# Value products placed after half a chunk more, both heads' probabilities in one tile, and a planner that repeats itself by latest times

## The chip, the cores and the metric

One Trainium2 core (of a chip with eight) runs the whole program. The metric is the device time of one execution in microseconds (us); lower is better.

## The reference

Sliding-window attention with a few global keys feeds a two-layer network with ELU between the layers; everything is 32-bit on input and output (the weights arrive as 64-bit numbers).

```python
scores = q @ k.T / sqrt(64) - slope[h] * dist        # B=4, H=8, S=768, D=64
keep   = (key < 8) | (0 <= query - key < 96)
a      = softmax(where(keep, scores, -1e9))
x      = concat_heads(a @ v)                          # 3072 x 512
h      = x @ w_in                                     # 512 -> 2048
g      = where(h > 0, h, exp(min(h, 0)) - 1)
out    = g @ w_out                                    # 2048 -> 512
```

## The kernel before, in words

**Tiling.** The 3072 tokens are twelve groups of 256, counted 0 to 11. A group has four head pairs for attention. The inner width 2048 is sixteen chunks of 128. Groups 0 to 2 run the network chunk by chunk while the weights are being converted (`moe`, L679), and groups 0 to 3 run attention in plain fp32 (`pair32`, L619). From group 3 on the network goes through `moe7` (L752): eight double chunks, each with an "up" (24 products of 128x256, L747, an accumulator of one PSUM bank) and a "down" (21 products, L808, seven block products in place of eight, each in three passes). `w_in` is streamed again from DRAM for each group, four loads of 512 KB in a period, through SP's queue into a ring of four slots.

**Split numbers.** Operands are split in a high part (rounded to fp32r) and a low part (the rest), so that two passes follow every tile: a copy (L282 when on ACT, L284 elsewhere) and a subtraction (`minus`, L290). All of them show the lines of these helpers, so the tile name tells them apart.

**The steady stretch.** While groups 3 to 10 run the network, attention of groups 4 to 11 is done beside it, one pair in a period of two double chunks (`pair`, L427). For pair k the steps are:
- load of q, v (`rqv`, L459) and keys (`rk`, L460), one buffer each;
- split of q (`qs`: ACT L482, DVE L484), of the keys (`ks`) and of v (`vd`: GpSimd L284 and L290). `vd` has two slots, so `vd` of pair k+2 waits for the value products of pair k; and as it is the last reader of `rqv`, the next load of `rqv` waits for it;
- a "visit" (L567), one unit on TensorE: the transposes of pair k-1 (L525, into the banks `t` and `th`) and the scores of pair k (L505, into the banks s0 and s1);
- softmax: mask and row maximum on DVE (L594, it frees the banks s0 and s1), exp on ACT (L596), the sum's reciprocal on DVE (L609, L610), scaling on DVE (L582);
- after the transposes: `pt`, high part on ACT (L282) and low part on DVE (L290), for each of two banks and two heads: four passes each;
- value products (L554), eight in a pair; their result goes through `x` (ACT L282, DVE L561) into `xh`.

The banks s0 and s1 hold in turn the accumulator of the even up, of the odd up and the two score tiles, so an up waits for the softmax of the visit ahead of it and a visit for the ELU passes (ACT L675, L676, DVE L677) of the ups.

**Order.** A planner, `Plan.order` (L106), lists every unit for every engine at build time, from costs written beside the units (`act`, `dve`, `pool`, L215 to L231) and a model of load times (`BW`, `LAT`, L62). An engine takes what can start now, the earliest `due` first. Where a unit has several engines (`alts`), the one that ends it first is taken. A flag `port` keeps certain DVE passes and all GpSimd passes from overlapping in the plan. Units with a `seq` run on TensorE exactly in the order of that number. On the chip each engine runs its list strictly in order, waiting where an input is late. In the steady stretch the numbers are offsets in a period of 13200 (constants at L914): up of the even chunk 0, values 2890, up of the odd chunk 3840, down of the previous odd chunk 6730, visit 9250, down of the even chunk 10650.

**End of a group.** When the last down of a group is done, `fin` (L824 to L830) gathers its four accumulators; the next group's first down writes the same banks.

The change touches `Op`, `Plan.add`, two new methods of `Plan`, `pair`, `inverse`, `norm`, `moe7`, `build`, the constants and `run`.

Of the kernel before, what the change touches and what calls it, by code (L numbers as in the profile page):

```python
# [53 lines left out]
class Op:  # L54
    __slots__ = ("room", "alts", "emit", "reads", "writes", "due", "n", "deps", "outs", "ready", "eng", "start", "end", "allocs", "uses", "bytes", "slack", "floor", "seq")


class Plan:
# [16 lines left out]
    def add(self, alts, emit, reads=(), writes=(), due=0.0, after=(), nbytes=0, slack=0.0, floor=0.0, seq=None):  # L75
# [11 lines left out]
        op.deps = len(deps)  # L87
# [16 lines left out]
    BY_DUE = ("S",)  # L104

# [113 lines left out]
def act(n, psum=False, extra=0.0):  # L219
    return (("ACT", (55 if psum else 97) + 0.834 * n + extra, False),)  # L220
# [14 lines left out]
class Kernel:  # L235
# [191 lines left out]
    def pair(self, b, gi, hp, xh, xl, due, ahead, step, X):  # L427
# [54 lines left out]
        p.add(act(W), lambda e: nc.scalar.activation(qs.t[:, HI], q32(), AF.Copy, scale=sc), [rqv], [qs], ahead - 4000)  # L482
# [8 lines left out]
        p.add(pool(nv, False), lambda e: self.copy(e, vv()[:, :, 0::3, :], v32()[:, v0:]), [rqv], [vd], due - 8000, self.parted)  # L491
        p.add(pool(nv), lambda e: self.minus(e, vv()[:, :, 1:3, :], v32()[:, v0:], vv()[:, :, 0::3, :]),
# [20 lines left out]
        self.inverse(st, ahead + 4500 + 3 * step)  # L513
# [13 lines left out]
        def rest():  # L527
            pts = [self.sb("pt", "pt", [P, 2 * NT, 2, P], F32R) for _ in range(2)]
            d = due - 2000
            for x, tp in enumerate(tps):  # L530
                r = slice(64 * x, 64 * x + 64)
                for j, pt in enumerate(pts):
                    if t0:
                        cut = [(slice(0, HK), slice(0, 4))]
                    else:
                        cut = [(slice(0, kr), slice(2 * i + a0, 2 * i + 2)) for i, (_, _, _, a0, kr, _) in enumerate(tiles)]
                    for rows, c in cut:
                        n = (c.stop - c.start) * 64
                        src = lambda j=j, tp=tp, rows=rows, c=c: tp.t[rows, 4 * j + c.start:4 * j + c.stop]
                        hi = lambda pt=pt, rows=rows, c=c, r=r: pt.t[rows, c, HI, r]  # L540
                        lo = lambda pt=pt, rows=rows, c=c, r=r: pt.t[rows, c, LO, r]
                        p.add(act(n, True), lambda e, src=src, hi=hi: self.copy(e, hi(), src()), [tp], [pt], d + 2 * x + j)
                        p.add(dve(n), lambda e, src=src, hi=hi, lo=lo: self.minus(e, lo(), src(), hi()), [tp, pt], [pt], d + 500 + 2 * x + j)
            self.after = []
# [3 lines left out]
            for j, pt in enumerate(pts):  # L548
                pv = self.bank("pv", "pv", [P, NT, 2, P])

                def values(e, j=j, pt=pt, pv=pv):
                    for i, (_, _, _, a0, kr, _) in enumerate(tiles):
                        for a in range(a0, 2):
                            nc.tensor.matmul(pv.t[:, i].rearrange("p s w -> p (s w)"), vd.t[:kr, 2 * i + a, j].rearrange("p s d -> p (s d)"),  # L554
                                             pt.t[:kr, 2 * i + a].rearrange("p s w -> p (s w)"), start=a == a0, stop=a == 1)

                self.after.append(p.add((("PE", 119.0 * sum(2 - x[3] for x in tiles), False),), values, [vd, pt], [pv], due + j, slack=0.0 if X.get("seven") else self.BEHIND, seq=due + j if X.get("seven") else None))
                r, o = head[j], head[1 - j]
                p.add((("ACT", 385.0, False),), lambda e, pv=pv, r=r, o=o: self.copy(e, xt(r), pv.t[o, :, 0]), [pv], [x], due + 500 + j)
                for y in range(2):  # L560
                    p.add(dve(W), lambda e, pv=pv, r=r, y=y: nc.vector.tensor_tensor(xt(r), pv.t[r, :, y], xt(r), ALU.add), [pv, x], [x], due + 600 + 2 * y + j)  # L561
            p.add(act(W), lambda e: self.copy(e, xh.t[:, HI, hp], x.t), [x], [xh], due + 700)
            p.add(pool(W), lambda e: self.minus(e, xh.t[:, LO, hp], x.t, xh.t[:, HI, hp]), [x, xh], [xl], due + 800)
# [41 lines left out]
    def inverse(self, st, due):  # L605
        nc = self.nc
# [5 lines left out]
        self.plan.add((("DVE", 290.0, False),), inverse, [st], [st], due)  # L612

    def norm(self, pr, lo, st, i, due, both):
        n = WN - lo
        self.plan.add((act(n, extra=90) + pool(n, False) if both else ()) + (("DVE", 130 + 0.53 * n, True),), lambda e: self.scaled(
            e, pr.t[:, lo:], pr.t[:, lo:], st.t[:, 2, i:i + 1]), [pr, st], [pr], due)

    def pair32(self, b, hp, t0, q32, k32, v32, rqv, rk, pv, due, step, X):  # L619
# [20 lines left out]
        self.inverse(st, d - 3500)  # L640
# [111 lines left out]
    def moe7(self, rows, xh, xl, up_at, down_at):  # L752
# [8 lines left out]
        def up(c, d):  # L761
            h = self.bank("S", "h", [P, 2, W], self.LAST_H if final and c >= N7 - 2 else None)
            for j in range(2):
# [6 lines left out]
                self.three(h, lambda j=j: h.t[:, j], w1, xh, xl, d + 10 * j, True)  # L770
            z = self.sb("z", "z", [P, 8, P], slots=["xh2"] if rows == self.GS * W and c == 1 else None)
            e = d + 2800
# [4 lines left out]
            any_ = lambda n: dve(n, port=True)  # L777
            tt = lambda e, out, x, y, op: self.on(e).tensor_tensor(out, x, y, op)  # L778
# [5 lines left out]
            ends = dve(3 * P, port=True) if final and c >= N7 - 2 else ()  # L784
            p.add(pool(3 * P) + ends, lambda e: self.minus(e, gg.t[:, LO, :3], z.t[:, 1:4], gg.t[:, HI, :3]), [z, gg], [low[0]], e)
# [32 lines left out]
        e = down_at[-1] - 4000  # L818
        fin = self.sb("fin", "fin", [P, 8, half], slots=["xh2"])
        lower = p.tile(None, "lower", None)  # L820
# [3 lines left out]
        p.add(act(DM, True), lambda _: nc.scalar.copy(f(5, 2), acc[0].t.rearrange("p i w -> p (i w)")), [acc[0]], [fin], e)  # L824
        p.add(dve(DM), lambda _: v(fin.t[:, 0:2], acc[1].t, twice(6), ALU.add), [acc[1], fin], [fin], e + 1)
        p.add(dve(DM), lambda _: v(fin.t[:, 2:4], acc[2].t, twice(0), ALU.add), [acc[2], fin], [fin], e + 2)
        p.add(dve(half), lambda _: v(f(4), acc[2].t[:, 0], f(3), ALU.add), [acc[2], fin], [lower], e + 3)
        p.add(dve(half), lambda _: v(f(3), f(3), f(5), ALU.subtract), [fin], [lower], e + 4)
        p.add(act(half, True), lambda _: nc.scalar.copy(f(7), acc[3].t[:, 0]), [acc[3]], [fin], e + 2)  # L829
        p.add(dve(half), lambda _: v(f(2), f(7), f(2), ALU.add), [fin], [fin], e + 5)  # L830
        end = down_at[-1] + 3000
        self.store(rows + P, [fin], lambda: f(1, 2), end)
        self.store(rows, [fin, lower], lambda: f(3, 2), end, final)

    def build(self):
# [52 lines left out]
        for (n, f0, f1), d in zip(segs, dues):  # L888
            def moe(n=n, f0=f0, f1=f1, d=d):
                b, gi = groups[n]  # L890
                rows = b * self.S + gi * W
                if n >= self.GS:
                    period = lambda c: d[0] + c // 2 * self.PERIOD
                    if n == len(groups) - 1:
# [5 lines left out]
                              [period(c) + (self.PERIOD + self.DOWN if c % 2 else self.VISIT + 1400.0) for c in range(self.NF7)])  # L900
# [7 lines left out]
        for _, f in sorted(todo, key=lambda x: x[0]):  # L908
# [5 lines left out]
    PERIOD, SECOND, DOWN, VISIT, AFTER = 13200.0, 3840.0, 6730.0, 9250.0, 20040.0  # L914
# [7 lines left out]
    ATT = {0: (0.0, 20000.0), 1: (20000.0, 36000.0), 2: (36000.0, 56000.0)}  # L922
# [5 lines left out]
             "pr": ["pr0", "pr1", "pr2", "pr3"], "st": [f"st{i}" for i in range(6)], "pt": ["pt0", "pt1"],  # L928
# [278 lines left out]
```

## Time and profile before

| | |
|---|---|
| three runs, median (lowest to highest) | 708.02 us (704.05 to 709.47) |
| the profiled execution, own time | 704.28 us |
| its span, first to last instruction | 702.5 us |
| TensorE busy, share of the span | 664.3 us, 95% |
| VectorE (DVE) | 588.1 us, 84% |
| ScalarE (ACT) | 483.4 us, 69% |
| GpSimd (POOL) | 293.3 us, 42% |
| bytes moved by DMA | 137.75 MB, 196 GB/s |

The rows below come from this execution. "x8" behind a row is a count; in a timeline neighbours of one kind are merged into one row. A bracket such as [1.42 <-DVE pt L290] is the idle time of the engine just before the instruction and what ended it. PEld is TensorE's weight load, SPq the queue of SyncE that issues loads and stores. PEclk is the granted TensorE clock as a share of full speed.

### The profile page before, as it was taken

The page shows a single profiled execution, that of the slowest core. Times are in us where ns is not written, and L with a number is a line of the kernel's source. Part 1 is how long each engine was busy: PE and PEld are TensorE (multiplying, and loading weights), DVE is VectorE, ACT ScalarE, POOL GpSimd, SP SyncE. Part 2 cuts the span into 40 slices and gives each one's busy share as a digit, 9 for nine tenths or more (in the row PEclk, how much of TensorE's full clock was granted, in tenths as well). Part 3 has the DMA queues.
Part 4 walks back from the last instruction along what each step waited for, and adds up shares of the span by engine and source line. Part 5 has one row for each costly group of instructions (what it writes and reads, how often), then busy time and mean ns, then how long its engine had stood idle before and what let it go on. Part 6 is the DMA issues. An engine that isn't in the chain of part 4 may idle for free.

```text
span 702.5 us, 16143 instructions
## 1 busy us (share of the span) xinstructions
PE 664.3 (95%) x5710; PEld 616.6 (88%) x5710; DVE 588.1 (84%) x1699; ACT 483.4 (69%) x1324; POOL 293.3 (42%) x307
## 2 busy tenths in 40 slices
PE   8999999999999998999999999999999899999995
PEld 6778888888789988999899889989998899989995
DVE  8999999999999879878778798787978887976644
ACT  7998887757686766567667576766767667765442
POOL 3152000203335544554455545444554455445440
PEclk9999999999999999999999999999999999999998
DMA  7838949311187564665656656755764766555651
GB/s 259 297 101 308 377 177 385 139 41 42 50 254 235 182 184 162 223 222 191 203 176 197 223 160 223 242 175 195 241 208 155 225 195 222 187 168 193 221 171 35
DMA packets 47627, 137.75 MB, mean 196 GB/s; under 512 B 5170, under 2 KB 14130, under 8 KB 47538
## 3 DMA queue, kind: packets, MB, share of 16 engines
q1 hardware_dynamic: 47248, 136.24, 57.6%
q8 instruction: 47, 0.77, 0.4%
q10 hardware_dynamic: 290, 0.39, 0.2%
q14 instruction: 42, 0.34, 0.1%
HBM read 119.84 MB, written 16.78 MB: 194 GB/s over the span
## 4 chain that ended last, share of the span: by engine, by line
PE 48%; DVE 20%; DMA 15%; ACT 12%; issue 3%; POOL 1%; SPq 1%; ACTq 0%; DVEq 0%; POOLq 0%
PE h L747 22%; DMA rqv<-in_qkv_dram 14%; PE a L808 12%; ACT pr L596 5%; PE o L705 4%; PE pv L554 4%; DVE pt L290 3%; DVE st L609 2%; ACT pt L282 2%; DVE pr L594 2%; DVE z L778 1%; PE s L505 1%; DVE g L409 1%; DVE gl L290 1%; DVE g L387 1%
## 5 line engine op out<-in xcount | busy, mean ns | idle before, releaser
L290 POOL TENSOR_TENSOR gg<-z,gg 128x384 fp32r<-128x384 f32 (+1 forms) x140 | 166.7, 1201 | 147.1 <-ACT gg L282 145.0
L747 PE MATMUL h<-xh,w0s 128*128 128x256 f32 x1728 | 218.4, 283 | 0.2
L747 PEld LDWEIGHTS h<-xh,w0s 128*128 128x128 f32 x1728 | 211.6, 192 | 0.8 <-DVE nmax L594 0.8
L808 PE MATMUL a<-w,gg 128*128 128x256 f32 x864 | 140.2, 277 | 0.1
L282 ACT CAST gg<-z 128x384 fp32r<-128x384 f32 (+1 forms) x144 | 81.2, 565 | 56.1 <-DVE z L677 32.5
L808 PEld LDWEIGHTS a<-w,gg 128*128 128x128 f32 x864 | 118.8, 188 | 0.4 <-ACT fin L829 0.3
L778 DVE TENSOR_TENSOR z<-z 128x128 f32<-128x128 f32 (+1 forms) x216 | 98.3, 456 | 3.0
L596 ACT ACTIVATE pr<-pr,nmax 128x232 f32<-128x232 f32 (+1 forms) x192 | 90.4, 472 | 14.8 <-DVE nmax L594 14.8
L747 PEld LDWEIGHTS h<-xh,w 128*128 128x128 f32 x576 | 82.2, 189 | 9.7 <-issue 1.7
L747 PE MATMUL h<-xh,w 128*128 128x256 f32 x576 | 89.0, 285 | 0.2
L594 DVE CUSTOM_DVE_ANT_0 pr<-s,tab 128x232 f32<-128x232 f32 (+1 forms) x192 | 64.6, 374 | 28.8 <-PE s L505 28.7
L677 DVE SCALAR_TENSOR_TENSOR z<-z,h 128x512 f32<-128x512 f32 x72 | 49.3, 685 | 34.1 <-ACT z L676 15.6
L675 ACT ACTIVATE z<-h 128x512 f32<-128x512 f32 x72 | 43.0, 598 | 49.6 <-PE h L747 47.4
L808 PE MATMUL a<-ta,gg 128*128 128x256 f32 x432 | 71.5, 277 | 0.0
L554 PE MATMUL pv<-pt,vd 116*128 116x256 f32 (+1 forms) x240 | 40.8, 297 | 23.1 <-DVE pt L290 22.3
L705 PE MATMUL o<-w,gh 128*128 128x512 f32 x192 | 59.4, 401 | 1.3 <-DVE ob L732 0.5
L561 DVE TENSOR_TENSOR x<-pv,x 64x256 f32<-64x256 f32 x128 | 53.8, 421 | 7.9 <-ACT x L282 4.8
L808 PEld LDWEIGHTS a<-ta,gg 128*128 128x128 f32 x432 | 59.3, 188 | 0.2 <-ACT gg L282 0.2
L554 PEld LDWEIGHTS pv<-pt,vd 116*128 116x128 f32 (+1 forms) x240 | 32.4, 190 | 29.7 <-issue 14.5
L808 PE MATMUL a<-tb,gg 128*128 128x256 f32 x216 | 50.0, 292 | 0.0
L582 DVE TENSOR_SCALAR pr<-pr,st 128x232 f32<-128x232 f32 (+1 forms) x143 | 47.3, 388 | 0.2
L584 POOL TENSOR_SCALAR pr<-pr,st 128x232 f32<-128x232 f32 (+1 forms) x31 | 17.2, 566 | 71.2 <-PE o L705 25.9
(131 smaller groups left out, 1169.3 us busy)
## 6 DMA issues: line engine op xcount, KB each, us to landing
w0s<-kept SPq DMA_DIRECT2D x144, 512.0 KB, 4.5
rqv<-in_qkv_dram SPq DMA_DIRECT2D x45, 384.0 KB, 4.7
rk<-in_qkv_dram SPq DMA_DIRECT2D x45, 184.0 KB, 3.2
bits<-in_w_in_dram SPq DMA_DIRECT2D x16, 512.0 KB, 6.5
bits<-in_w_out_dram SPq DMA_DIRECT2D x16, 512.0 KB, 9.1
kept<-w SPq DMA_DIRECT2D x16, 512.0 KB, 5.3
out_dram<-fin SPq DMA_DIRECT2D x17, 256.0 KB, 2.4
kept<-w SPq DMA_DIRECT2D x8, 256.0 KB, 5.2
```

The lines of the kernel that those rows point to most:

```text
L282: self.nc.scalar.copy(out, x)
L290: self.on(e).tensor_tensor(out, x, y, ALU.subtract)
L554: nc.tensor.matmul(pv.t[:, i].rearrange("p s w -> p (s w)"), vd.t[:kr, 2 * i + a, j].rearrange("p s d -> p (s d)"), pt.t[:kr, 2 * i + a].r ...
L561: p.add(dve(W), lambda e, pv=pv, r=r, y=y: nc.vector.tensor_tensor(xt(r), pv.t[r, :, y], xt(r), ALU.add), [pv, x], [x], due + 600 + 2 * y + j)
L582: self.nc.vector.tensor_scalar(out, x, sc, None, ALU.mult)
L594: p.add((("DVE", 158 + 1.042 * n, False),), lambda e: nc.vector.tensor_tensor_reduce(pr.t[:, lo:], st_()[:, lo:], tab, -(2.0 ** -(h + 1)), ...
L596: p.add(act(n, extra=200), lambda e: nc.scalar.activation(pr.t[:, lo:], pr.t[:, lo:], AF.Exp, bias=nm, scale=-1.0, accum_out=st.t[:, 0, i: ...
L677: p.add(dve(n), lambda e: nc.vector.scalar_tensor_tensor(out(), out(), -1.0, hx(), ALU.add, ALU.max), [h, ex], [ex], due)
L705: nc.tensor.matmul(acc[i].t, g.t[:, i * P:(i + 1) * P], w2.t[:, s], start=fc == f0 and n == 0 and s == HI, stop=fc == f1 - 1 and n == 1)
L747: self.nc.tensor.matmul(hx(), w1.t[:, s, cc * P:(cc + 1) * P], xh.t[:, x, cc], start=n == 0 and cc == 0, stop=n == 2 and cc == self.NCC - 1)
L778: tt = lambda e, out, x, y, op: self.on(e).tensor_tensor(out, x, y, op)
L808: nc.tensor.matmul(acc[i].t[:, j], gg.t[:, x, g], w(s), start=c == x == s == 0 and n in (0, 2, 4, 6), stop=c == N7 - 1 and x == LO and n i ...
```

## The change

**The order on TensorE.** In a period the offsets become: up even 0, first half of up odd 2890, values 4335, second half of up odd 5280, down of the previous odd chunk 6730, first six products of down even 9250, visit 9255, the other fifteen products of down even 9260 to 9280. So value products come behind the first half of the odd chunk instead of ahead of it, and the visit comes six products later.

**The planner.** It runs three times. Between the runs `latest` goes back from the end through the order just made, on a TensorE line without any idle time, and gives each unit that is not on TensorE, has no `seq` and starts after 195 us its latest time as its new `due`.

**Units.** The transposed probabilities of both heads share one tile, so a pair has two copies and two subtractions of 512 columns in place of four and four of 256 (in a batch's first group the number also halves). The high part of `vd` may go to ACT and its low part to DVE; the first low part of a down's operand may go to DVE; a pair's scaling may go to ACT. The addition ahead of the reciprocal goes from DVE to ACT. The attention of group 3 gets a due window of its own (80 to 135 us; by the old rule 58 to 170.8 us), and `fin` is tracked in finer parts with an earlier due time.

```diff
+    def latest(self, out, since):
...
+        for op in reversed(out):
+            end = far
+            for o in op.outs:
+                end = min(end, o.late - (self.SEM + self.LAT[op.eng] if o.eng != op.eng else 0.0))
+            for v in op.uses:
+                if v in after:
+                    end = min(end, after[v].late - self.SEM - self.LAT[op.eng])
+            op.late = min(end - cost(op) - (self.LANDS if op.bytes else 0.0), ideal.get(op, far))
+        for op in out:
+            if op.seq is None and op.eng != "PE" and op.start > since:
+                op.due = op.late
+        self.again()
+    LANDS = 1500.0
...
-        p.add(pool(nv, False), lambda e: self.copy(e, vv()[:, :, 0::3, :], v32()[:, v0:]), ...
-        p.add(pool(nv), lambda e: self.minus(e, vv()[:, :, 1:3, :], ...
+        p.add(pool(nv, False) + act(nv), lambda e: self.copy(e, vv()[:, :, 0::3, :], v32()[:, v0:]), ...
+        p.add(pool(nv) + dve(nv, port=True), lambda e: self.minus(e, vv()[:, :, 1:3, :], ...
...
-            pts = [self.sb("pt", "pt", [P, 2 * NT, 2, P], F32R) for _ in range(2)]
-            d = due - 2000
+            pt = self.sb("pts", "pt", [P, 2, 2 * NT, 2, P], F32R)
+            d = due - 6000
...
-                self.after.append(p.add(... values, [vd, pt], [pv], due + j, ... seq=due + j if X.get("seven") else None))
+                self.after.append(p.add(... values, [vd, pt], [pv], due + j, seq=due + j))
-                p.add((("ACT", 385.0, False),), ... [pv], [x], due + 500 + j)
+                p.add((("ACT", 275.0, False),), ... [pv], [x], due - self.ASAP + j)
...
+        p.add((("ACT", 200.0, False),), lambda e: nc.scalar.activation(st.t[:, 1], st.t[:, 0], AF.Copy, bias=1e-9), [st], [st], due)
+        p.add((("DVE", 100.0, False),), lambda e: nc.vector.reciprocal(st.t[:, 2], st.t[:, 1]), [st], [st], due)
...
-        self.plan.add((act(n, extra=90) + pool(n, False) if both else ()) + (("DVE", 130 + 0.53 * n, True),), ...
+        more = act(n, extra=90) + pool(n, False) if both else act(n)
+        self.plan.add(more + (("DVE", 130 + 0.53 * n, True),), ...
...
-                self.three(h, lambda j=j: h.t[:, j], w1, xh, xl, d + 10 * j, True)
+                self.three(h, lambda j=j: h.t[:, j], w1, xh, xl, d + (10.0 if final or c % 2 == 0 else self.SPLIT) * j, True)
...
-            p.add(pool(3 * P) + ends, lambda e: self.minus(e, gg.t[:, LO, :3], ...
+            p.add(pool(3 * P) + any_(3 * P), lambda e: self.minus(e, gg.t[:, LO, :3], ...
...
-                              [... self.VISIT + 1400.0) for c in range(self.NF7)])
+                              [... self.DOWN2) for c in range(self.NF7)])
...
-    PERIOD, SECOND, DOWN, VISIT, AFTER = 13200.0, 3840.0, 6730.0, 9250.0, 20040.0
+    PERIOD, SECOND, SPLIT, DOWN, DOWN2, VISIT, VALUES = 13200.0, 2890.0, 2390.0, 6730.0, 9250.0, 9255.0, 4335.0
+    AFTER = 2 * PERIOD - VISIT + VALUES
+    ASAP = 3000.0
+    PASSES, SINCE = 2, 195000.0
-    ATT = {0: (0.0, 20000.0), 1: (20000.0, 36000.0), 2: (36000.0, 56000.0)}
+    ATT = {3: (80000.0, 135000.0), 0: (0.0, 20000.0), 1: (20000.0, 36000.0), 2: (36000.0, 56000.0)}
...
         order = self.plan.order(self.slots())
+        for _ in range(self.PASSES):
+            self.plan.latest(order, self.SINCE)
+            order = self.plan.order(self.slots())
```

## Rows read from the trace of the kernel before

**Rows 1.** Stretches: PE, PEld, DVE, ACT, POOL busy, PEclk, DMA share, GB/s.

```profile
60.00:200.02 140.02, 138.05 (x947) 119.75 (x946) 136.25 (x348) 105.81 (x286) 26.91 (x31) 1.00 0.53 194
200.02:635.65 435.63, 412.12 (x3839) 395.76 (x3838) 360.80 (x1066) 298.00 (x824) 223.19 (x216) 0.99 0.61 201
635.65:695.05 59.40, 59.29 (x519) 58.86 (x518) 33.65 (x72) 27.98 (x53) 23.30 (x22) 1.00 0.49 159
```

**Rows 2.** PE's waits: for whom, us in total, times, longest.

```profile
PE pv L554 <- DVE pt L290: 22.3, 29, 1.6
```

**Rows 3.** Single periods, transposes to transposes, columns as in rows 1.

```profile
200.02:213.09 13.07, 12.87 (x107) 11.38 (x107) 12.88 (x38) 10.22 (x29) 6.08 (x7) 1.00 0.79 254
622.85:635.65 12.80, 12.80 (x127) 12.56 (x126) 9.94 (x30) 8.86 (x23) 6.41 (x7) 1.00 0.49 159
254.28:271.50 17.22, 14.87 (x129) 14.27 (x128) 12.53 (x31) 9.38 (x25) 8.46 (x9) 0.90 0.57 185
```

**Rows 4.** Stretches around a stall in the period at 254.28, columns as in rows 1.

```profile
262.00:264.00 2.00, 0.71 (x4) 0.52 (x4) 1.83 (x5) 1.98 (x6) 1.44 (x1) 1.00 0.50 162
266.00:268.00 2.00, 2.00 (x11) 2.00 (x11) 1.97 (x4) 0.41 (x1) 2.00 (x3) 0.50 0.00 0
```

**Rows 5.** Timeline of one visit and the value products behind it.

```profile
400.46 0.91 PE L505 MATMUL s<-ks,qs 64*128 64x232 f32 x12
400.69 0.65 ACT L282 CAST pt<-t 116x256 fp32r<-116x256 f32 x2
403.74 0.51 ACT L482 ACTIVATE qs<-rqv,scale 128x256 fp32r<-128x256 f32 x1 [2.41 <-DMA rqv<-in_qkv_dram]
403.80 2.99 PE L747 MATMUL h<-xh,w0s 128*128 128x256 f32 x24
...
407.23 0.35 ACT L282 CAST pt<-th 116x256 fp32r<-116x256 f32 x1
408.52 0.39 DVE L290 TENSOR_TENSOR pt<-th,pt 116x256 fp32r<-116x256 f32 x1
409.06 0.71 PE L554 MATMUL pv<-pt,vd 116*128 116x256 f32 x4 [1.42 <-DVE pt L290]
```

**Rows 6.** Waits of the other engines, columns as in rows 2.

```profile
POOL vd L284 <- PE pv L554: 51.6, 30, 2.9
...
DVE pr L594 <- PE s L505: 28.7, 20, 1.7
...
ACT qs L482 <- DMA rqv<-in_qkv_dram: 24.2, 20, 3.2
```

**Rows 7.** Timeline: end of a group's last down, and its gathering.

```profile
384.35 0.57 ACT L824 COPY fin<-a 128x512 f32<-128x512 f32 x1
384.62 0.84 PE L808 MATMUL a<-w,gg 128*128 128x256 f32 x6
385.16 0.69 DVE L825 TENSOR_TENSOR fin<-a,fin 128x512 f32<-128x512 f32 x1
```

**Rows 8.** Groups by shape: count, busy us, mean ns, idle before.

```profile
L290 POOL TENSOR_TENSOR vd<-rqv,vd 128x512 fp32r<-128x512 f32 x24 | 31.7, 1319 | 1.9
...
L609 DVE TENSOR_SCALAR st<-st 128x4 f32<-128x4 f32 x48 | 20.2, 421 | 8.0 <-ACT pr L596 7.6
L290 DVE TENSOR_TENSOR pt<-t,pt 116x256 fp32r<-116x256 f32 x48 | 18.9, 413 | 1.6 <-ACT pt L282 1.6
...
L290 DVE TENSOR_TENSOR gg<-z,gg 128x384 fp32r<-128x384 f32 x2 | 1.1, 551 | 0.0
```

**Rows 9.** Timeline: a GpSimd subtraction and a DVE subtraction that overlap.

```profile
376.54 1.48 POOL L290 TENSOR_TENSOR gg<-z,gg 128x512 fp32r<-128x512 f32 x1 [1.53 <-ACT gg L282]
...
376.79 1.63 DVE L290 TENSOR_TENSOR ks<-rk,ks 128x368 fp32r<-128x368 f32 x1
```

**Rows 10.** Timeline: late softmax of the visit whose scores run to 272.88.

```profile
275.60 0.39 DVE L594 CUSTOM_DVE_ANT_0 pr<-s,tab 128x232 f32<-128x232 f32 x1
...
276.05 2.57 PEld L747 LDWEIGHTS h<-xh,w0s 128*128 128x128 f32 x22 [0.34 <-DVE nmax L594]
```

More of the change, by code (lines that the diff above doesn't have):

```diff
@@ L54 @@
 class Op:
-    __slots__ = ("room", "alts", "emit", "reads", "writes", "due", "n", "deps", "outs", "ready", "eng", "start", "end", "allocs", "uses", "bytes", "slack", "floor", "seq")
+    __slots__ = ("room", "alts", "emit", "reads", "writes", "due", "n", "deps", "outs", "ready", "eng", "start", "end", "allocs", "uses", "bytes", "slack", "floor", "seq", "need", "late")
 class Plan:
@@ L86, in add @@
             deps.update(v.readers)
-        op.deps = len(deps)
+        op.deps = op.need = len(deps)
         op.outs, op.ready, op.eng = [], {}, None
@@ L104, with again @@
     BY_DUE = ("S",)
+    def again(self):
+        for op in self.ops:
+            op.deps, op.ready, op.eng = op.need, {}, None
+            for v in op.uses:
+                v.left, v.slot, v.free_at = 0, None, 0.0
+        for op in self.ops:
+            for v in op.uses:
+                v.left += 1
+    def latest(self, out, since):
+        after, held = {}, {}
+        for op in out:
+            for v in op.allocs:
+                if v.slot in held:
+                    after[held[v.slot]] = op
+                held[v.slot] = v
+        line = [op for op in out if op.eng == "PE"]
+        cost = lambda op: next(a[1] for a in op.alts if a[0] == op.eng)
+        at = None
+        ideal = {}
+        for op in line:
+            at = op.start if at is None or op.start < since else at
+            ideal[op] = at
+            at += cost(op)
+        far = out[-1].start
+        for op in reversed(out):
+            end = far
+            for o in op.outs:
+                end = min(end, o.late - (self.SEM + self.LAT[op.eng] if o.eng != op.eng else 0.0))
+            for v in op.uses:
+                if v in after:
+                    end = min(end, after[v].late - self.SEM - self.LAT[op.eng])
+            op.late = min(end - cost(op) - (self.LANDS if op.bytes else 0.0), ideal.get(op, far))
+        for op in out:
+            if op.seq is None and op.eng != "PE" and op.start > since:
+                op.due = op.late
+        self.again()
+    LANDS = 1500.0
     def order(self, slots):
@@ L823, in moe7 @@
         twice = lambda k: fin.t[:, k:k + 1].broadcast_to([P, 2, half])
[L824 to L830, printed above, removed]
+        begin = p.add(act(DM, True), lambda _: nc.scalar.copy(f(5, 2), acc[0].t.rearrange("p i w -> p (i w)")), [acc[0]], [fin], e)
+        p.add(dve(DM), lambda _: v(fin.t[:, 0:2], acc[1].t, twice(6), ALU.add), [acc[1], fin], [first], e + 1)
+        p.add(dve(DM), lambda _: v(fin.t[:, 2:4], acc[2].t, twice(0), ALU.add), [acc[2], first], [second], e + 2)
+        p.add(act(half, True), lambda _: nc.scalar.copy(f(7), acc[3].t[:, 0]), [acc[3]], [spare], e + 2, after=[begin])
+        p.add(dve(half), lambda _: v(f(4), acc[2].t[:, 0], f(3), ALU.add), [acc[2], second], [lower], e + 3)
+        p.add(dve(half), lambda _: v(f(3), f(3), f(5), ALU.subtract), [second], [lower], e + 4)
+        p.add(dve(half), lambda _: v(f(2), f(7), f(2), ALU.add), [spare, second], [upper], e + 5)
         end = down_at[-1] + 3000
-        self.store(rows + P, [fin], lambda: f(1, 2), end)
+        self.store(rows + P, [fin, first, upper], lambda: f(1, 2), end)
         self.store(rows, [fin, lower], lambda: f(3, 2), end, final)
```

71 lines of the change are left out of this document (36 added, 35 removed).

## The prediction, made before the changed kernel was run

> **What bounds the kernel now.** I read the stretches first. From 60 to 200 us PE is busy for 138.1 of 140.0 us and from 635.65 to the last product for 59.3 of 59.4 [rows 1]: there the kernel is bound by products, and the change takes none away. The stretch between them, from the first to the last of 32 visits, is the one to look at: 435.63 us for 31 periods, 14.05 us each, and PE idle for 23.5 us of it. DVE is busy there for 360.8 us, 11.64 in a period, ACT for 9.61, POOL for 7.20 [rows 1]; none of them fills 14.05 us.
>
> Then I read PE's own waits. One line holds nearly all: the value products waited for the low part of `pt` 29 times, 22.3 us in total, at most 1.6 [rows 2]. What a period costs without that wait is seen in single periods. Eleven of the 31 have at most 0.2 us of PE idle; they average 13.15 us (12.79 to 13.84, worked out from the timeline of each; the first and the last of them stand in [rows 3]). So the stretch carries 435.63 - 31 x 13.15 = 28 us that the products don't need. 22.3 is the wait itself. 3.2 more is the clock: in two periods (that at 254.28 is one) PE's busy time alone is 14.87 and 14.74 us where a neighbour has about 13.2 [rows 3], because after idle stretches (0.71 us busy in the two from 262 us) the granted clock is 0.50, the lower of its two levels, 1.2 GHz [rows 4]. The other 2.5 us are restarts where the eight value products run in two halves.
>
> Why `pt` is late is seen in the timeline [rows 5]. The transposes are done when the scores begin, at 400.46. ACT copies the bank `t` at once (400.69), but the bank `th`, ready at the same time, only at 407.23 at last, because ahead of it in ACT's list stands `qs`, which waits 2.41 us for its load, and the four exps. DVE's last subtraction starts at 408.52, PE goes on at 409.06. ACT waits for that load 20 times, 24.2 us in all [rows 6]. It is no data dependence of the values; it is the order in ACT's list. The load is late because `rqv` is freed by `vd`, and GpSimd's `vd` waits for the value products of two pairs before (51.6 us, 30 times) [rows 6]: the stall feeds itself from pair to pair.
>
> **The change part by part.**
>
> *Place of the values.* From the end of the scores to the value products PE now has 21 products of the down (from the scores' end at 401.37 to the up at 403.80, 2.43 us) and one up of 24 (2.99), 5.42 us [rows 5]. After, it has 15/21 of the down (1.74) and 36 products of an up and a half (4.48), 6.22 us: 0.80 us more time for `pt`. The mean wait is 22.3/29 = 0.77 [rows 2], the one of 1.42 [rows 5] keeps 0.62. So the place alone takes away between 13 us (the longest keep up to 0.8 of their 1.6) and all of the 22.3.
>
> *Order by latest times.* `pt` is needed 6 us after the scores, the exps only by the next transposes, 13 us on; by latest times both copies of `pt` go ahead of the exps and of `qs`. Then `th` is copied behind `t`, at about 401.9 in the timeline of [rows 5] in place of 407.23; DVE's subtractions, behind its four softmax passes, are done by 401.37 + 4 x 0.39 + 2 x 0.69 = 404.3 (their lengths: [rows 7, 10]) against values at 407.6. That leaves some 3 us, and I take the wait as gone but for 0.2 us a period (order made from modelled times, run with real ones). The wait of `qs` for its load stays in ACT's list, but with exps behind it that have 10 us of room; what hides it is ACT's own idle time, 14.05 - 9.61 = 4.4 us a period [rows 1]; uncovered it would be 24.2/31 = 0.8 us a period [rows 6].
>
> *What the values are moved past.* Half an up, so its result and the odd chunk's ELU come at the same place as before; the ring slot of the odd chunk's second load is freed 1 us later, and SP's queue, strictly in order, holds the next `w_in` loads and the `rqv` and `rk` loads behind it. `vd` of pair k+2 starts later by the same 1.4 us (half an up), so `rqv` is issued later; but `vd` on ACT and DVE would take about 0.57 + 0.69 us (other passes of 512 columns on the two, [rows 7]) where GpSimd's low part alone takes 1.32 [rows 8]. I set this at zero; its bounds are +0.8 us a period (the wait of `qs` grown through to PE) and -0.1.
>
> *Passes merged and moved.* Two subtractions of 256 columns at 0.41 [rows 8] against one of 512 at 0.69 [rows 7]: 0.13 us a bank, 0.25 a period off DVE; on ACT 0.65 for two [rows 5] against 0.57 [rows 7], 0.16 a period. The addition for the reciprocal, 0.42 us on DVE with its waits [rows 8], goes to ACT, where a pass on four columns has no row of before: between 0.1 (its DVE work alone) and 0.65 (twice a pass of 256 columns); I take 0.2. The low part of a down's operand costs 0.55 on DVE [rows 8], twice a period, of `vd` 0.69; scalings may go the other way. DVE stays within 11.0 to 12.9 us of a 13.35 us period. No PE time hangs on these as long as DVE keeps 0.4 us free.
>
> What a move to DVE can cost is seen in one overlap: a subtraction of 368 columns took 1.63 us while GpSimd's subtraction ran from 376.54 to 378.02, and ended 0.4 after it [rows 9]. The Trainium skill, page "SBUF — State Buffer", section "Who interferes with whom", says that a DVE instruction with two SBUF inputs contends with a GpSimd instruction that reads SBUF and that the loser blocks fully. By that rule, which the overlap bears out, each pass moved from GpSimd to DVE is one that can block; by it the sum would be that of the rival "DVE becomes the bound" below, 703; without it, the 684 below.
>
> *End of a group.* The down of the old group is now followed at once by six products of the new one, into the same banks; before, a visit lay between. ACT's copy of the first bank is done at 384.92, DVE's read of the second at 385.85, the old down ends at about 385.4; the third pair of new products, which writes the second bank, comes 0.47 us later [rows 7]. So 0 to 0.6 us at 8 group ends; I take 0.2, 1.6 us.
>
> *Group 3's attention, the finer `fin`.* The first lies where PE is busy for 98.6% [rows 1]: -2 to +3 us, taken as zero. The second: 0 to -0.5 us, zero.
>
> **Sum.** 31 x (14.05 - 13.15) = 28 us gone, less 31 x 0.2 = 6.2 kept, less 1.6 at group ends: 20.2 us. The span becomes 682.3; the profiled execution lies 1.78 us above its span (704.28 to 702.5): 684 us. The three runs have their median at 708.02, 3.7 above the profiled execution. I take it that a kernel that waits less also spreads less, and leave 684 as it is.
>
> **The rivals.**
>
> *The wait shrinks by half.* If the plan still thinks that the load lands early and puts `qs` ahead of a copy of `pt`, only the place helps: 13 of the 22.3 us and half of the clock's 3.2: 704.3 - 14 = 690. For it: the same load model. Against: one copy for both heads leaves only one instruction that can be behind.
>
> *Nothing is left.* 28 us go and the stretch before 200 us gives its 2 us: 674. For it: periods of 13.07 and 12.80 us exist [rows 3].
>
> *DVE becomes the bound.* 11.64 now, plus 0.55 x 2 + 0.69 for what may be moved to it, plus one block of 1.04 us (1.63 [rows 9] less 0.59, which 368 columns take at the 0.41 of 256 [rows 8]), less 0.25 and 0.42: 13.8 us, and with 0.2 us of waits 14.0, as before: 703. Against: the moves are choices of the plan, which takes the engine that ends first.
>
> *Slower: the up waits for the softmax.* The even up needs the bank s0, which DVE frees with its first two passes. PE came 2.43 us after the scores [rows 5]; now it comes after 15 products, 1.74. Mostly DVE is waiting for the scores (20 times, 28.7 us [rows 6]) and starts at once. But in the period at 271.97 the second pass ended at 275.99, 3.1 us after the scores' end, and the weight load was held by it [rows 10]. If DVE came that late in each period, PE would wait 3.1 - 1.74 = 1.36: 13.15 + 1.36 = 14.51 us, 0.46 more than now, in 31 periods 14 us: 718. It decides from 13.15 + w = 14.05: passes that end later than 2.6 us after the scores in the mean.
>
> **How the numbers follow.** Forecast 0.55 (676 to 690 by itself), half 0.18, nothing left 0.11, DVE bound 0.08, slower 0.08. The range of 8 in 10 goes from 672 (nothing left, and 2 us more by the early stretch) to 699 (the half case with 0.3 us a period of its unknown costs). Within 1% is what a measurement here can hardly tell from no change; against 708.02 that is 701 to 715. Faster: the first three and a little loss, 0.83; same 0.09; slower 0.08.
>
> **What would show it.** Right: visits 13.3 to 13.4 us apart; the value products' wait for `pt` under 8 us in total; copies of `th` ahead of the exps; no stretch in the middle with a granted clock of 0.5. Wrong: a new line in PE's waits (an up for the row maximum, the first products of a down for `fin` or for `gg`); DVE over 12.8 us in a period; `qs` still ahead of `pt` in ACT's list.

## The result: 3.7% faster, and what the profile shows after

The changed kernel takes 681.18 us (median of 4 runs, 680.14 to 684.46) against 708.75 us beside it (704.05 to 709.86): a ratio of 0.9631, 95% interval 0.9576 to 0.9686. The forecast was 684, with a range of 672 to 699. The profiled execution's span fell by 22.8 us, from 702.5 to 679.7; the medians differ by 27.6, because the profiled execution of the kernel before, 704.28 us, is near its fastest and its other runs go up to 709.86. The stretches of the changed kernel, columns as in [rows 1]:

```profile
60.00:197.89 137.89, 136.88 (x945) 118.87 (x943) 135.25 (x353) 107.83 (x294) 18.33 (x25) 1.00 0.55 201
197.89:613.61 415.72, 407.19 (x3853) 394.65 (x3852) 370.54 (x972) 331.74 (x861) 126.44 (x120) 1.00 0.62 211
613.61:673.10 59.49, 58.60 (x513) 58.17 (x512) 33.25 (x81) 27.39 (x50) 14.20 (x13) 1.00 0.46 152
```

The 31 periods from visit to visit shrink from 435.63 us [rows 1] to 415.72, 19.9 us or 87% of the whole; a period is 13.41 us. The first visit comes 2.1 us sooner, what lies behind the last is 0.8 us shorter. PE is idle for 8.5 us between the visits, where it was idle for 23.5. In a period DVE is busy for 11.95 us (11.64 before), ACT for 10.70 (9.61), GpSimd for 4.08 (7.20).

PE's waits in the changed kernel, columns as in [rows 2]:

```profile
PE th L566 <- DVE x L601: 5.8, 7, 1.0
...
PE pv L594 <- DVE pt L331: 0.7, 1, 0.7
```

The 22.3 us of [rows 2] are 0.7. A new line is at the top: the transposes wait for DVE's last pass over the value products, whose banks they write. Single periods after, columns as in [rows 3]; the first and the third don't wait, the second has that new wait:

```profile
213.38:226.44 13.06, 13.06 (x128) 12.82 (x127) 10.66 (x32) 9.61 (x25) 2.54 (x3) 1.00 0.62 217
266.20:280.42 14.22, 13.18 (x128) 12.73 (x127) 13.07 (x36) 10.59 (x28) 4.39 (x5) 1.00 0.60 215
440.14:453.21 13.07, 13.07 (x128) 12.82 (x127) 11.41 (x28) 10.50 (x28) 3.88 (x5) 1.00 0.57 192
```

No stretch like that of 266 us in [rows 4] is left, the granted clock of the whole stretch reads 1.00 where it read 0.99. A visit of the changed kernel and the value products behind it, to be read beside [rows 5]:

```profile
373.70 0.93 PE L546 MATMUL s<-ks,qs 64*128 64x232 f32 x12
373.93 0.59 ACT L323 CAST pt<-t 116x512 fp32r<-116x512 f32 x1 [0.35 <-PE th L566]
...
376.16 0.49 ACT L636 ACTIVATE pr<-pr,nmax 128x232 f32<-128x232 f32 x1 [0.98 <-DVE nmax L634]
...
376.65 0.50 ACT L523 ACTIVATE qs<-rqv,scale 128x256 fp32r<-128x256 f32 x1
...
377.05 0.56 ACT L323 CAST pt<-th 116x512 fp32r<-116x512 f32 x1
...
377.81 0.68 DVE L331 TENSOR_TENSOR pt<-th,pt 116x512 fp32r<-116x512 f32 x1
...
380.70 1.12 PE L594 MATMUL pv<-pt,vd 116*128 116x256 f32 x8
```

The copy of `th` starts 2.4 us after the scores' end; before, the second of its two copies started 5.9 us after it [rows 5]. `pt` is done at 378.5, 2.2 us ahead of its use. But one exp, the copy of the keys and `qs` still stand ahead of the copy of `th`. Over all visits two of the four exps stand ahead of it in the mean (all four before), and `qs` in 29 of 31, as before: it isn't the list that the prediction drew.

### The profile page after: what moved, and what is told of

Its sections match the earlier page's. It is cut to its first block, busy times and chain, and to the rows that moved or that the text cites. A ratio compares the mean times of both kernels' runs of the same rounds, so it can differ in the third digit from the quotient of the medians.

```text
span 679.7 us, 15993 instructions
## 1 busy us (share of the span) xinstructions
PE 657.4 (97%) x5710; PEld 613.8 (90%) x5710; DVE 595.0 (88%) x1613; ACT 517.5 (76%) x1362; POOL 178.2 (26%) x195
## 4 chain that ended last, share of the span: by engine, by line
PE 72%; DVE 15%; ACT 5%; DMA 4%; issue 2%; POOL 0%; DVEq 0%; ACTq 0%; POOLq 0%; SPq 0%
PE h L792 32%; PE a L853 21%; PE o L750 6%; DMA rqv<-in_qkv_dram 4%; PE pv L594 4%; PE s L546 3%; DVE x L601 2%; PE t L566 2%; PE s L678 2%; PE pv L712 1%; PE t L695 1%; ACT pr L636 1%; DVE g L450 1%; DVE gl L331 1%; PE th L566 1%
## 5 line engine op out<-in xcount | busy, mean ns | idle before, releaser
L792 PE MATMUL h<-xh,w0s 128*128 128x256 f32 x1728 | 215.2, 281 | 0.0
L792 PEld LDWEIGHTS h<-xh,w0s 128*128 128x128 f32 x1728 | 208.1, 190 | 0.6
L331 POOL TENSOR_TENSOR gg<-z,gg 128x512 fp32r<-128x512 f32 x70 | 91.7, 1310 | 269.5 <-issue 134.1
L323 ACT CAST gg<-z 128x384 fp32r<-128x384 f32 (+1 forms) x144 | 81.2, 565 | 27.0 <-DVE z L824 13.4
L824 DVE TENSOR_TENSOR z<-z 128x128 f32<-128x128 f32 (+1 forms) x216 | 83.8, 388 | 2.0
L853 PE MATMUL a<-ta,gg 128*128 128x256 f32 x432 | 75.0, 285 | 0.0
L331 DVE TENSOR_TENSOR gg<-z,gg 128x384 fp32r<-128x384 f32 x74 | 72.4, 979 | 1.1 <-ACT gg L323 0.4
L853 PE MATMUL a<-tb,gg 128*128 128x256 f32 x216 | 47.0, 279 | 0.7 <-DVE part L772 0.7
L721 ACT ACTIVATE z<-z 128x512 f32<-128x512 f32 x72 | 45.3, 629 | 1.3
L620 ACT ACTIVATE pr<-pr,st 128x232 f32<-128x232 f32 (+1 forms) x99 | 43.6, 469 | 1.2 <-DVE st L650 1.2
L750 PEld LDWEIGHTS o<-w,gh 128*128 128x128 f32 x192 | 32.1, 189 | 6.1 <-ACT gh L323 1.1
```

What stands on the lines that cost most here:

```text
L323: self.nc.scalar.copy(out, x)
L331: self.on(e).tensor_tensor(out, x, y, ALU.subtract)
L620: self.nc.scalar.activation(out, x, AF.Copy, scale=sc)
L721: p.add(act(n), lambda e: nc.scalar.activation(out(), out(), AF.Exp, scale=-1.0), [ex], [ex], due)
L750: nc.tensor.matmul(acc[i].t, g.t[:, i * P:(i + 1) * P], w2.t[:, s], start=fc == f0 and n == 0 and s == HI, stop=fc == f1 - 1 and n == 1)
L792: self.nc.tensor.matmul(hx(), w1.t[:, s, cc * P:(cc + 1) * P], xh.t[:, x, cc], start=n == 0 and cc == 0, stop=n == 2 and cc == self.NCC - 1)
```

## The experiments

Twelve kernels, each timed beside the kernel before on the same chip; "alone" means one part put into the kernel before, "taken back" one part undone in the changed kernel. They were timed in three sessions on three chips, in which the kernel before took 706.13, 708.74 and 705.98 us. So where two experiments are set against each other, a difference of some 3 us isn't clear of noise.

### The place alone

```diff
-    PERIOD, SECOND, DOWN, VISIT, AFTER = 13200.0, 3840.0, 6730.0, 9250.0, 20040.0
+    PERIOD, SECOND, SPLIT, DOWN, DOWN2, VISIT, VALUES = 13200.0, 2890.0, 2390.0, 6730.0, 9250.0, 9255.0, 4335.0
+    AFTER = 2 * PERIOD - VISIT + VALUES
...
+                self.three(h, lambda j=j: h.t[:, j], w1, xh, xl, d + (10.0 if final or c % 2 == 0 else self.SPLIT) * j, True)
```

> The kernel before with the new offsets alone (values behind the first half of the odd up, six products of the down ahead of the visit); costs, dues, units and a single plan as before. Theory 'order' (the copies of the bank th stand behind a load and the exps in ACT's list): 0.8 us more time a period takes 13 of the 22.3 us of waits, 690 to 697 us, and the value products' wait for pt stays at 5 to 10 us. Rival 'place' (the 0.8 us are all that matters): 682 to 687 us, wait under 4. Rival 'engines' (the gain comes from passes moved off GpSimd and DVE): over 700 us.

Measured: 710.37 us, ratio 1.0082 (1.0042 to 1.0123), a little slower. Of the three only "engines" (over 700) fits the time, "order" fits the wait, nearly. PE's waits:

```profile
PE pv L554 <- DVE pt L290: 11.7, 10, 1.7
PE h L747 <- DVE nmax L594: 10.7, 16, 1.5
```

The wait for `pt` shrank by 10.6 us, less than the 13 that the prediction's step gave it at least. (The passes that make `pt` are due 2 us ahead of the values, so their due times move with the place by 1.4 us; this run doesn't separate the two.) Nearly the same, 10.7 us, came back as the even up waiting for the row maximum, the mechanism of the "slower" rival: the place takes from the softmax what it gives to `pt`. One such place in this kernel's timeline (the scores ran to 273.3):

```profile
273.20 2.44 POOL L290 TENSOR_TENSOR gg<-z,gg 128x512 fp32r<-128x512 f32 x2 [0.88 <-ACT gg L282]
273.26 1.52 DVE L778 TENSOR_TENSOR z<-z 128x256 f32<-128x256 f32 x1
...
274.71 1.22 DVE L830 TENSOR_TENSOR fin<-fin 128x256 f32<-128x256 f32 x1
275.85 0.39 DVE L594 CUSTOM_DVE_ANT_0 pr<-s,tab 128x232 f32<-128x232 f32 x1
...
276.37 0.39 DVE L594 CUSTOM_DVE_ANT_0 pr<-s,tab 128x232 f32<-128x232 f32 x1
...
276.82 4.35 PE L747 MATMUL h<-xh,w0s 128*128 128x256 f32 x36 [1.52 <-DVE nmax L594]
```

The lines ahead of the softmax say why it is late. Two DVE passes that take 0.41 us each by themselves take 1.52 and 1.22 us while GpSimd's two subtractions run, 1.9 us more together, and PE waits for 1.52. In all 16 of these waits DVE passes between the scores and the up are stretched by 1.6 to 2.1 us in this way, and the waits are 0.2 to 1.5 us long. The late softmax of [rows 10] has the same pass ahead of it; from the kernel before:

```profile
273.78 2.45 POOL L290 TENSOR_TENSOR gg<-z,gg 128x512 fp32r<-128x512 f32 x2 [5.07 <-ACT gg L282]
273.84 1.52 DVE L778 TENSOR_TENSOR z<-z 128x256 f32<-128x256 f32 x1
```

So the price of the place depends on what GpSimd does at that moment. The changed kernel with GpSimd's passes put back (below) has this wait again, 9.5 us; the changed kernel has none. The order counts too: with a single plan the changed kernel has 8.7 us of it.

### The copies put first by hand

```diff
-            d = due - 2000
+            d = due - 6000
```

> The kernel before with one number changed: the copies and subtractions that make pt are due 4 us earlier, so that both banks are copied ahead of the exps. Values stay at their old place. 'Order': the wait for pt falls from 22 to under 8 us, 684 to 692 us, and ACT's wait for the load of rqv stays (over 15 us in total) without holding PE. 'Place': under 1% of gain, 702 us or more. 'Engines': the same, 702 or more.

Measured: 724.17 us, ratio 1.0229 (1.0158 to 1.03). PE's waits:

```profile
PE s L505 <- DVE z L677: 11.2, 9, 1.7
PE h L747 <- DVE nmax L594: 8.4, 4, 2.8
PE th L525 <- DVE x L561: 5.4, 9, 1.4
PE pv L554 <- DVE pt L290: 3.0, 6, 0.8
```

The wait for `pt` went to 3.0 us, as "order" expected, and the kernel became 2.3% slower, which only the other two allow: three other consumers of DVE's list are late in its place, 25.0 us together. And the lateness now comes in lumps. Two periods of this kernel with such lumps and one without:

```profile
227.93:246.58 18.65, 16.61 (x127) 15.98 (x127) 12.51 (x38) 10.87 (x28) 8.76 (x9) 0.82 0.48 148
277.83:295.23 17.40, 15.02 (x127) 14.43 (x126) 13.64 (x38) 10.24 (x28) 8.16 (x9) 0.90 0.59 211
295.23:308.04 12.81, 12.81 (x127) 12.56 (x127) 9.33 (x31) 8.98 (x24) 5.91 (x7) 1.00 0.54 180
```

Two us of waiting in one period go with a mean granted clock of 0.82 and 0.90 in that period, and PE is busy for 16.61 and 15.02 us with work that takes 12.8 to 13.2. Inside the first of them, all engines:

```profile
228.00:230.00 2.00, 0.97 (x17) 0.67 (x17) 1.94 (x5) 1.39 (x3) 0.94 (x2) 1.00 0.59 225
234.00:236.00 2.00, 2.00 (x12) 2.00 (x11) 1.80 (x9) 2.00 (x7) 0.35 (x1) 0.50 0.01 4
```

PE is busy for about half of 228 to 232 us, then without a break, but at a granted clock of 0.50, the level of 1.2 GHz as in [rows 4]. Nine periods have a mean below 0.97 here, two in the kernel before.

### The split of q planned later

```diff
-        p.add(act(W), lambda e: ... scale=sc), [rqv], [qs], ahead - 4000)
+        p.add(act(W), lambda e: ... scale=sc), [rqv], [qs], ahead - 4000, slack=3500.0)
```

> The kernel before with the split of q planned 3.5 us later than its inputs are modelled to be there, so that it doesn't stand waiting for its load in ACT's list. 'Order': ACT's wait for rqv falls from 24 to under 6 us and the wait for pt with it to about half, 688 to 697 us (the exps still stand ahead of the copies of th). 'Place' and 'engines': 702 us or more.

Measured: 704.89 us, ratio 0.9981 (0.9946 to 1.0015): no difference, against "order". ACT's wait for the load of `rqv`, 24.2 us in [rows 6], has no line any more. PE's first line:

```profile
PE pv L554 <- DVE pt L290: 17.3, 34, 2.6
```

In one visit whose scores end at 403.56:

```profile
407.47 0.62 ACT L282 CAST pt<-th 116x256 fp32r<-116x256 f32 x2
```

`qs` now comes behind these copies, at 407.99, but they start 3.9 us after the scores all the same: the four exps, the copy of the keys and a copy of `gg` stand ahead of them. Over all visits the last copy of `th` starts 4.9 us after the scores in the mean, 5.1 in the kernel before. So the wait that stood in front of the copies in [rows 5] was not by itself what made them late; without it the list fills with something else.

### The repeated plan alone

```diff
+        for _ in range(self.PASSES):
+            self.plan.latest(order, self.SINCE)
+            order = self.plan.order(self.slots())
```

> The kernel before with the plan repeated twice by latest times, nothing else. 'Order': the latest times put the copies ahead of the exps; 683 to 692 us, wait for pt under 8 us. 'Place': 695 us or more, since without the 0.8 us a wait of 0.5 us a period stays. 'Engines': 700 or more.

Measured: 694.38 us, ratio 0.9835 (0.9767 to 0.9902). That lies between "order" (up to 692) and "place" (from 695); but the wait for `pt` is gone without the place, so "place" has its reason wrong. PE's first line, and that of the values:

```profile
PE s L546 <- DVE z L718: 7.5, 13, 1.1
...
PE pv L595 <- DVE pt L331: 1.5, 3, 0.5
```

And the scalings by shape, from 200 to 610 us, in this kernel and in the kernel before:

```profile
L623 DVE TENSOR_SCALAR pr<-pr,st 128x232 f32<-128x232 f32 x108 | 73.2, 709 | 1.0
...
L582 DVE TENSOR_SCALAR pr<-pr,st 128x232 f32<-128x232 f32 x100 | 34.5, 397 | 0.1
```

A scaling takes 0.71 us here, 0.40 in the kernel before, and 0.33 to 0.34 in both where GpSimd does nothing beside it. The latest times move it nearer to the transposes (4.0 us from its end to them in the median, 5.4 before), and there 80 of 108 scalings overlap a pass of GpSimd, against 18 of 108 before.

### The changed kernel with a single plan

```diff
-    PASSES, SINCE = 2, 195000.0
+    PASSES, SINCE = 0, 195000.0
```

> The changed kernel with a single plan (no repeat by latest times). Theory 'latest times' (the four runs so far: hand-set dues only move the lateness from one consumer of DVE's and ACT's lists to the next, latest times spread it): as with the place alone the up waits for the row maximum, 8 us or more, or another line does; 698 to 712 us. Rival 'units' (merged and moved passes make room enough on DVE for any order): under 690 us.

Measured: 696.73 us, ratio 0.9823 (0.9747 to 0.99), just under the range of "latest times" and far from that of "units". The repeated plan is worth 15.5 us in the changed kernel. PE's first line is the one of the place alone, the up waiting for the row maximum:

```profile
PE h L792 <- DVE nmax L634: 8.7, 18, 1.0
```

### The changed kernel with the old place

```diff
-    PERIOD, SECOND, SPLIT, DOWN, DOWN2, VISIT, VALUES = 13200.0, 2890.0, 2390.0, 6730.0, 9250.0, 9255.0, 4335.0
-    AFTER = 2 * PERIOD - VISIT + VALUES
+    PERIOD, SECOND, DOWN, VISIT, AFTER = 13200.0, 3840.0, 6730.0, 9250.0, 20040.0
```

> The changed kernel with the old offsets (values ahead of the odd up, the visit ahead of the whole even down). 'Latest times': the values hardly wait for pt (under 3 us), but the scores, which come 0.7 us earlier, wait for the ELU of the odd chunk as in the kernel with the plan repeated alone (7.5 us there): 684 to 690 us. Rival 'place' (values need the 0.8 us): wait for pt over 6 us, over 690. If the place is worth nothing beside the latest times: 681 to 683.

Measured: 680.29 us, ratio 0.9603 (0.9532 to 0.9674), no different from the changed kernel within the intervals. The third case is the nearest: beside the other parts the place is worth nothing. The values wait 1.2 us for `pt`, the scores 1.0 for the ELU. And the line of the load of `rqv` in the waits of all engines is nearly that of [rows 6]:

```profile
ACT qs L523 <- DMA rqv<-in_qkv_dram: 22.8, 24, 2.0
```

22.8 us of that wait in a kernel of 680 us, none in one of 705: it doesn't set the time.

### The choice of engines taken back

```diff
-        p.add(pool(nv, False) + act(nv), ...
-        p.add(pool(nv) + dve(nv, port=True), ...
+        p.add(pool(nv, False), ...
+        p.add(pool(nv), ...
...
-        more = act(n, extra=90) + pool(n, False) if both else act(n)
+        more = act(n, extra=90) + pool(n, False) if both else ()
...
-            p.add(pool(3 * P) + any_(3 * P), ...
+            p.add(pool(3 * P) + (any_(3 * P) if ends else ()), ...
```

> The changed kernel with the choice of engines taken back (v's split and the down's first low part on GpSimd alone, a pair's scaling on DVE alone); latest times, place, merged passes and the sum's addition on ACT stay. 'Latest times': 683 to 688 us, GpSimd busy about 290 us again. Rival 'units': 692 us or more. The rival of the prediction that moved passes block each other by the shared port: 678 to 680, faster without them.

Measured: 725.72 us, ratio 1.0232 (1.0157 to 1.0306): 44.5 us slower than the changed kernel. By the profiled executions it is 44.1 us: PE is idle for 23.5 us more, and busy for 20.6 us longer with the same 5710 products, since the granted clock between the visits is 0.97 in the mean where it is 1.00 in the changed kernel. PE's first line:

```profile
PE t L566 <- DVE pr L622: 26.0, 36, 1.7
```

And its timeline at one visit:

```profile
398.13 2.56 POOL L331 TENSOR_TENSOR gg<-z,gg 128x384 fp32r<-128x384 f32 x2
...
398.24 2.59 DVE L622 TENSOR_SCALAR pr<-pr,st 128x232 f32<-128x232 f32 x3
...
400.88 0.27 PE L566 MATMUL t<-ident,pr 64*116 64x64 f32 x1 [0.93 <-DVE pr L622]
```

Three scalings, 0.33 us each when nothing is beside them, take 2.59 us while GpSimd's two passes run, and the transposes stand behind them. The first and the third of them begin during a GpSimd pass and end 0.14 us after it (GpSimd's end at 399.18 and 400.69, the scalings at 399.32 and 400.83). The Trainium skill, page "SBUF — State Buffer", section "Who interferes with whom", says that a `tensor_scalar` may use a mode that takes the port pair which DVE shares with GpSimd, and that whichever issues first has it for its whole instruction while the other is blocked. The trace agrees with it: 2.59 us beside 2.56, with ends 0.14 us behind GpSimd's.

### Place and repeated plan together, no unit changed

The edits of the first and the fourth experiment in the kernel before.

> The kernel before with the new offsets and the repeated plan, no unit changed. 'Latest times': place costs nothing here and helps the scores: 683 to 689 us, the wait of the up for the row maximum under 3 us (10.7 with the place alone). Rival 'units': 694 us or more, since DVE is too full for the shorter way from the scores to the even up.

Measured: 709.28 us, ratio 1.0028 (0.9983 to 1.0073). "Latest times" fails: with the old units the place takes back all that the repeated plan gives. The up's wait for the row maximum is gone, as it expected, but PE's first line is now the scaling, as in the experiment before:

```profile
PE t L566 <- DVE pr L623: 19.5, 28, 2.0
```

### The choices one by one

With the scaling on DVE alone (the `more` line of the seventh experiment) in the changed kernel:

> The changed kernel with one choice taken back: a pair's scaling runs on DVE alone, as before; v's split and the down's low part keep their choices (GpSimd busy about 180 us). Theory 'scaling': with latest times the scaling is listed just ahead of the transposes, on DVE it is held there by GpSimd's pass, and PE waits: 700 us or more, transposes waiting for pr over 10 us. Rival 'GpSimd': the trouble is the time GpSimd holds the port, which these choices have cut: 681 to 687 us. If both are needed: between, 688 to 699.

Measured: 683.11 us, ratio 0.9644 (0.9591 to 0.9698), as "GpSimd" said, and no different from the changed kernel within the intervals. With v's split and the first low part on GpSimd alone (the other lines of it):

> The changed kernel with the other choice taken back: v's split and the down's first low part on GpSimd alone (busy about 290 us), the scaling free to go to ACT. 'Scaling': 680 to 687 us. 'GpSimd': 700 us or more, DVE passes stretched beside GpSimd's and PE waiting for one of them. If both are needed: 688 to 699.

Measured: 692.08 us, ratio 0.978 (0.9726 to 0.9833), between the two, in the range of "both are needed". PE waits for the row maximum:

```profile
PE h L792 <- DVE nmax L634: 9.5, 15, 1.2
```

The sums of the ELU output (`z<-z`, both inputs in SBUF) and the additions to `x` (one input in PSUM) by shape, from 200 to 610 us, in the changed kernel:

```profile
L601 DVE TENSOR_TENSOR x<-pv,x 64x256 f32<-64x256 f32 x122 | 51.3, 421 | 11.4 <-ACT x L323 8.7
L824 DVE TENSOR_TENSOR z<-z 128x128 f32<-128x128 f32 x120 | 46.5, 387 | 1.0
...
L824 DVE TENSOR_TENSOR z<-z 128x256 f32<-128x256 f32 x60 | 24.8, 414 | 0.0
```

and with v's split and the low part on GpSimd:

```profile
L824 DVE TENSOR_TENSOR z<-z 128x128 f32<-128x128 f32 x119 | 59.8, 512 | 1.5
L601 DVE TENSOR_TENSOR x<-pv,x 64x256 f32<-64x256 f32 x120 | 50.5, 421 | 12.1 <-ACT x L323 9.2
L824 DVE TENSOR_TENSOR z<-z 128x256 f32<-128x256 f32 x59 | 43.8, 742 | 1.5
```

The sums, with both inputs in SBUF, are stretched by a third and by four fifths; the additions that read PSUM keep their 421 ns. So the prices of the two choices don't add up: taken back by itself the one costs 1.9 us (within the noise), the other 10.9, both together 44.5. Either a scaling that can go elsewhere or a GpSimd that is mostly free keeps PE from the long wait. With neither, 57 of the 108 scalings on DVE between the first and the last visit overlap a pass of GpSimd; with only the scaling taken back it is 19 of 108, with only the others 2 of 52.

### The repeated plan and a free scaling in the kernel before

The edits of the fourth experiment and the `more` lines of the change.

> The kernel before with two things only: the plan repeated by latest times, and the scaling of a pair free to go to ACT. Place, merged passes, v's split, the sum's addition and group 3's window stay as before. 'Scaling': the two parts are most of the change, 680 to 687 us. 'GpSimd': about as with the repeated plan alone, 691 to 696.

Measured: 690.69 us, ratio 0.9754 (0.9698 to 0.9811): "GpSimd", just under its range. The scores' wait for the ELU is still 7.5 us. Freeing the scaling is worth 3.7 us beside the repeated plan; the intervals of the two overlap, so that isn't clear of noise.

### The passes over the value products sooner

In the changed kernel's worst kind of period the transposes stand behind `x`, which stands behind the gathering of a group's result:

```profile
371.98 0.69 DVE L871 TENSOR_TENSOR fin<-a,fin 128x512 f32<-128x512 f32 x1
372.70 0.43 DVE L601 TENSOR_TENSOR x<-pv,x 64x256 f32<-64x256 f32 x1
...
373.28 0.24 PE L566 MATMUL th<-ident,pr 64*116 64x64 f32 x1 [1.03 <-DVE x L601]
```

```diff
-                op.due = op.late
+                op.due = op.late - (2000.0 if op.writes[:1] and op.writes[0].name.startswith("x_") else 0.0)
```

> The changed kernel with the passes that read the value products out (tile x) due 2 us ahead of their latest time. If the 5.8 us that the transposes wait for x in the changed kernel are a matter of order: that line under 2 us and 675 to 679 us. If DVE is too full there, another line takes its place: 680 to 684.

Measured: 674.71 us (673.89 to 675.61), ratio 0.9534 (0.9482 to 0.9587): the fastest here, and apart from the changed kernel's 680.14 to 684.46 run by run. The line is gone; the first that is left in the middle is

```profile
PE a L853 <- DVE fin L870: 3.1, 6, 0.7
```

the next group's down waiting for the gathering of the last, the wait that the prediction priced at 0 to 0.6 us a time. From the first to the last visit (198.05 to 605.97 us) a period is now 13.16 us, what the waitless periods of the kernel before took.

## Why the prediction was right, and where its steps were wrong

**What bounds the kernel: right.** The gain came where the first view put it, 19.9 of 22.8 us between the visits, and the period of 13.15 us without waits, read from eleven single periods, is where the last experiment ends (13.16, with 0.14 us of idle time in it). Of the eleven periods ten have at most 0.2 us of idle time and one 0.23, which changes nothing. The clock's 3.2 us went with the waits: no period of the changed kernel has a mean below 0.97. That the other 2.5 us were restarts between the halves of the value products, no run shows. Of the signs, the visits are 13.41 us apart (13.3 to 13.4 expected), the wait for `pt` is 0.7 us (under 8) and no stretch has a clock of 0.5; but one sign of being wrong came too, `qs` ahead of `pt` in ACT's list.

**Place of the values: wrong.** The step gave it at least 13 us by itself. It took 10.6 us off the wait named, but as the rival of the slower side said, the even up then waits for the softmax, 10.7 us. Alone it costs 0.8%; beside the repeated plan with the old units it costs 14.9 us (709.28 to 694.38), there by way of the scaling; in the whole change it is worth nothing (680.29 without it). The price of the shorter way from scores to up stood in a rival; it belonged in this step's sum. And that rival took the late row maximum of [rows 10] as given: it was late behind a DVE pass of 1.52 us in place of 0.41, beside GpSimd, and with GpSimd's passes moved and the plan repeated PE has no such wait in the changed kernel.

**Order by latest times: right about the wait, wrong in its picture.** The wait for `pt` is down to 1.5 us without any new place, as the step said; the kernel gains 1.65% by it alone and 15.5 us in the changed kernel. But putting the copies first is not enough: done by hand it made the kernel 18 us slower, and in the changed list two exps in the mean and `qs` are still ahead of `th`. The latest times set all consumers of DVE and ACT against one another; in the two experiments by hand, a single one put first moved the lateness to the next.

**The wait of `qs` for its load: wrong as a cause.** The reading of the timeline stopped at the longest bracket in front of the late copy. Taken away, nothing changed (0.9981); nearly whole, the kernel ran at 680 us. Nor does the loop by way of `vd` hold: its wait for the values [rows 6] is 46.4 us in the changed kernel, 8.9 in the equally fast one with the old place.

**Passes merged and moved: wrong, by a term set at zero.** The step said that no PE time hangs on them as long as DVE keeps 0.4 us free. DVE's busy time hardly changed, as it said (11.95 us in a period, within its 11.0 to 12.9), and the choices are worth 44.5 us in the changed kernel. The block that it saw in one overlap [rows 9] was counted only against the change, as a cost of passes moved to DVE. The larger effect has the other sign: GpSimd, busy for 4.08 us a period in place of 7.20, holds up DVE's passes less, and the rival "DVE becomes the bound" (703) didn't come.

**End of a group: right**, 0.5 us in all in the changed kernel (1.6 expected), 3.1 in the last experiment. **Group 3's window**, set at zero: the first visit comes at 196.6 to 198.3 us in all kernels with it, at 199.9 to 202.3 in those without. That is some 2 us and only argued, since it was not tried by itself; nor were the merged tile, the sum's addition on ACT and the finer `fin`.

So the total was right partly by luck. The sum took the wait for `pt` as gone, and of the two reasons that it gave, one (the place, 13 us or more) is worth nothing in the change; what made room in its stead is a term that was set at zero (the engines). The wait that nobody priced, transposes for `x`, is 5.8 of the 8.5 us of idle time that were left.

## What to carry to other kernels

When a tensor engine waits for one late pass on a busy engine (DVE at 84% here), expect that moving that pass or its consumer by hand moves the lateness to the next consumer. What worked here was to give all passes of the list their latest times from an ideal line of the tensor engine, then a margin to the ones that still came late. Before just-in-time passes are put on DVE, look at what GpSimd does at that moment; a second engine for either of the two may be worth more than the busy times say. And take a bracket in front of a late instruction as a cause only after a run without it.

## What was not expected of the hardware

Waits that came in lumps cost more than their length. With the copies put first, PE is idle for 44.9 us of its span (723.5 less 678.6 busy) against 38.2 in the kernel before, 6.7 us more, but the span grew by 21: PE is busy for 14.3 us longer with the same 5710 products, in periods where the granted clock is 0.82 or 0.90 in the mean.

```profile
PE 678.6 (94%) x5710; PEld 632.3 (87%) x5710; DVE 584.9 (81%) x1698; ACT 484.0 (67%) x1324; POOL 291.4 (40%) x308
```
